# Attention and two feed-forward layers on one core: where the activation is made, and over how many units a weight's steps are spread

## The chip, the core and the metric

One core of a Trainium2 chip. It has five engines, each with an instruction queue of its own that is worked off in order: TensorE for matrix products (PE in the profile; PEld is its loading of weights), VectorE (DVE), ScalarE (ACT), GpSimd (POOL) and SyncE (SP, which here only issues transfers). Engines wait for one another by semaphores. TensorE writes to PSUM, in eight banks; all else lies in SBUF.

The metric is the device time of one execution in microseconds (us), lower being better. The kernel before was timed three times: 675.92, 677.68 and 681.2, median 677.68.

## The reference: what is computed

An attention of 2 batches, 12 heads, 448 tokens of 64, whose scores are mixed over the heads before the softmax and again after it, and then two feed-forward layers on the 896 tokens of 768:

```python
x = attn_out.transpose(0, 2, 1, 3).reshape(896, 768)
h = x @ w_in;  g = np.maximum(h, 0.0) + alpha * np.minimum(h, 0.0);  x = g @ w_out    # layer 1, d_ff 2048
h = x @ w_in2; g = np.maximum(0.01 * h, h);                          x = g @ w_out2   # layer 2
```

The weights arrive as float64, as two 32-bit words for each number, and are turned into float32 on the chip.

## The kernel before, in words

**Attention** takes the first 188 us of the profile. The order of its instructions on each engine is made by a planner (`Work`, with a table `STEPS` of costs and due times), which also places the first pieces of the feed-forward layers: the loading and splitting of the first weights and the first two output blocks of layer 1.

**Feed-forward** is worked in 80 units, written out in program order. A unit is one block of weights of 128 rows. Layer 1 has 16 up units (`u1_0` to `u1_15`, 768 columns, one block of 128 hidden features each, 36 matmuls of 448 tokens) and 24 down units (`d1_c_g`, 512 columns, 24 matmuls each; four of them make one output block `c` of 128 features); layer 2 has the same again. Each number is kept as a high part and a low part (`whi`, `wlo` for weights, `xhi`, `xlo` and `ghi`, `glo` for activations), and each product is made of three matmuls: `whi*xhi`, `whi*xlo`, `wlo*xhi`. In a group the first two kinds alternate (L449, L450), and the third kind follows (L452).

**The weights of a unit** need a load and seven steps, here called step 0 to step 6: the transfer `wraw` (L403, two buffers), step 0 on ScalarE (L418), steps 1 to 4 on VectorE (L420, L423, L425, L427), all in a working tile `wt` (two buffers), step 5 on ScalarE (L432), which makes `whi`, and step 6 on GpSimd (L435), which makes `wlo` (`whi` and `wlo` have two buffers). The same line serves up units (`wt_u`, 768 columns) and down units (`wt_d`, 512).

**The activation** of an up unit takes the sums `ps` (128x896, two banks of the four pairs of banks that take turns). In layer 1 VectorE makes `min(p,0)*alpha` into the tile `gt` (L606) and then adds `max(p,0)` (L608); in layer 2 ScalarE makes `0.01*p` (L610) and VectorE the maximum (L612). ScalarE then makes the high part `ghi` from `gt` (L614), GpSimd the low part `glo` (L615).

**The order around an up unit u**: VectorE gets the unit's own activation interleaved with steps 1 to 4 of unit u+2 (`prepare`), ScalarE its high part, step 0 of unit u+2 and step 5 of unit u+1, GpSimd step 6 of unit u+1 and `glo`, and SP the load of unit u+3. Steps 1 to 4 of unit u+2 and all that follows the matmuls of unit u stand in the same turn. In a down unit the group's matmuls stand ahead of the steps, and after each fourth one `to_y` (layer 1) or `to_out` (layer 2) takes the sums out.

Of the kernel before, what the change touches and what calls it, by code (L numbers as in the profile page):

```python
# [32 lines left out]
NCC, NFF = DM // 128, FF // 128  # L33
# [144 lines left out]
def tile_kernel(ctx: ExitStack, tc: tile.TileContext, qt, kt, vt, wmix, mmix,  # L178
# [3 lines left out]
    PE, DV, AC, PO, SP = nc.tensor, nc.vector, nc.scalar, nc.gpsimd, nc.sync  # L182
    PSUM = bass.MemoryType.PSUM

    const = ctx.enter_context(tc.tile_pool(name="const", bufs=1))
# [205 lines left out]
    raws, whl, wt = {}, {}, {}  # L391
# [5 lines left out]
    def load_w(e, u):  # L397
        if u >= len(units):
            return
        name, src = units[u]  # L400
        n = src.shape[-1]
        raw = pools["wp"].tile([128, 768, 2], I32, tag="wraw", name=f"wraw_{name}")
        e.dma_start(raw[:, :n], src.bitcast(I32).rearrange("p (n w) -> p n w", w=2))  # L403
        raws[u] = raw

    def split_w(e, u, i):

        if u >= len(units):
# [24 lines left out]
        if i == 6:  # L433
            hi, lo = whl[u]
            e.tensor_sub(lo[:, :n], t.bitcast(F32), hi[:, :n].bitcast(F32))  # L435

    SPLIT_ON = (AC, DV, DV, DV, DV, AC, PO)

    def three(p, whi, wlo, xhi, xlo, first, last):
        PE.matmul(p, whi, xhi, start=first, stop=False)  # L440
        PE.matmul(p, whi, xlo, start=False, stop=False)
        PE.matmul(p, wlo, xhi, start=False, stop=last)

    def group(p, whi, wlo, x, first, last):
# [38 lines left out]
    add(("load_mix",), 0, load_mix, wait=DMA)  # L483
    add(("clear",), 0, clear)
    add(("mixing",), 0, mixing, after=[("load_mix",)])

    for j, (b, t) in enumerate(tiles):
        start = first[j] - 20 if j else -40
        for c in range(NP2):
# [7 lines left out]
            p = "ps", "score", j, c  # L497
# [10 lines left out]
    for m, ks in enumerate(pairs):  # L508
        k0, k1 = ks[0], ks[-1]
        p, p2 = ("ps", "mix", m), ("ps", "post", m)  # L510
# [60 lines left out]
    def next_banks():  # L571
        n_bank[0] += 1
        return two_banks[in_turn[(n_bank[0] - 1) % NPS]]

    n_unit = [0]

    def prepare(i):

        u = n_unit[0]
        if i < 5:  # L580
            if u:
                split_w(SPLIT_ON[i], u + 2, i)
        elif u:
            if u > 1:
                split_w(SPLIT_ON[5], u + 1, 5)
                split_w(SPLIT_ON[6], u + 1, 6)
            load_w(SP, u + 3)

    def up(layer, x):
        g = []  # L590
        for f in range(NFF):
            whi, wlo = whl.pop(n_unit[0])
            ghi = gp.tile([128, B, S], F32R, tag=f"ghi{f}", name=f"ghi{layer}_{f}")
            glo = gp.tile([128, B, S], F32R, tag=f"glo{f}", name=f"glo{layer}_{f}")
            prepare(0)
            prepare(5)
            if layer == 1 and f in pu:
                p = pu[f]
            else:
                p = next_banks()  # L600
                for b in range(B):
                    group(p[:, b, :S], whi, wlo, list(zip(*x[b])), True, True)
            p = p[:, :, :S]
            t = gp.tile([128, B, S], F32, tag="gt", bufs=2, name=f"gt{layer}_{f}")
            if layer == 1:
                DV.tensor_scalar(t, p, 0.0, alpha_sb[:, f:f + 1], op0=ALU.min, op1=ALU.mult)  # L606
                prepare(1)
                DV.scalar_tensor_tensor(t, p, 0.0, t, op0=ALU.max, op1=ALU.add)  # L608
            else:
                AC.mul(t, p, 0.01)  # L610
                prepare(1)
                DV.tensor_max(t, p, t)  # L612
            prepare(2)
            AC.copy(ghi, t)  # L614
            PO.tensor_sub(glo, t, ghi.bitcast(F32))  # L615
            prepare(3)
            prepare(4)
            n_unit[0] += 1
            g.append((ghi, glo))
        return g  # L620

    def down(layer, g, done):
        for c in range(NCC):

            if layer == 2 and c == NCC - 1:
                p = [next_banks()[:, 0] for b in range(B)]
            else:
                both = next_banks()
                p = [both[:, b] for b in range(B)]
            for fg in range(4):  # L630
                whi, wlo = whl.pop(n_unit[0])
                prepare(5)
                for b in range(B):
                    group(p[b][:, :S], whi, wlo, [(hi[:, b], lo[:, b]) for hi, lo in g[4 * fg:4 * fg + 4]],
                          fg == 0, fg == 3)
                for part in range(5):
                    prepare(part)
                n_unit[0] += 1
            done(c, p)

    g = up(1, x)

    def to_y(c, p):
        for b in range(B):
            AC.copy(x[b][0][c], p[b][:, :S])
            DV.tensor_sub(x[b][1][c], p[b][:, :S], x[b][0][c].bitcast(F32))  # L646

    down(1, g, to_y)
    g = up(2, x)

    def to_out(c, p):
        o = gp.tile([128, B, S], F32, tag="gt", bufs=2, name=f"o_{c}")
        for b in range(B):
            AC.copy(o[:, b], p[b][:, :S])
            SP.dma_start(outT[128 * c:128 * c + 128, b * S:(b + 1) * S], o[:, b])
# [53 lines left out]
```

## Time and profile before

| | |
|---|---|
| median of three runs (lowest, highest) | 677.68 us (675.92, 681.2) |
| the profiled execution: its own time | 681.03 us |
| its span, first to last instruction | 679.0 us |
| PE busy | 644.0 us, 95% |
| DVE busy | 487.7 us, 72% |
| ACT busy | 273.8 us, 40% |
| POOL busy | 221.0 us, 33% |
| chain that ended last | PE 72%, DVE 19%, issue 4%, ACT 2% |
| TensorE's mean granted clock | 0.991 |

The profile is of one execution, by the chip's profiler. A busy share is an average over stages with different limits: the chain of waits, which is followed back from the last instruction, goes through PE nearly everywhere, but between 196 and 324 us, in the up units of layer 1, through DVE (the lines L606, L420, L425, L427). Matmuls overlap each other, so the start of one to the start of the next is what they cost, not the length of a row. In a row of the timeline the first number is the start in us from the span's start, the second the length; in brackets stands how long the engine had been idle before it and who ended that.

### The profile page before, as it was taken

To read this page: it belongs to the slowest core of one execution; us is meant where nothing else is said; L and a number is where in the kernel's file an instruction comes from. 1 tells how busy PE (TensorE), PEld (TensorE's weight loads), DVE (VectorE), ACT (ScalarE), POOL (GpSimd) and SP (SyncE) were. 2 spreads that over 40 slices of the span, in tenths; PEclk is the share of its full clock that TensorE was granted. 3 is DMA by queue.
4 is the path that set the end of the run, shared out by engine and by line. 5 is a ranking of instruction groups with operands and counts; after the bars stand their busy time and mean duration, and the time that the engine had idled before them with its cause. 6 is when DMAs were issued, how large, how long until landed. Compare 5 with 4: busy or idle time off the path is not lost.

```text
span 679.0 us, 14909 instructions
## 1 busy us (share of the span) xinstructions
PE 644.0 (95%) x6316; PEld 535.2 (79%) x6316; DVE 487.7 (72%) x589; ACT 273.8 (40%) x476; POOL 221.0 (33%) x174
## 2 busy tenths in 40 slices
PE   8879999999998888889899999999999999999997
PEld 3546656565797777778799999899899898999997
DVE  3758776788449999999666666667788776665651
ACT  4637656757323222222223232344454542323231
POOL 3101011102225444445323222245655553222221
PEclk9979999999999999999899999999999999999999
DMA  7668346333202222221333333422322323443430
GB/s 280 220 185 254 120 165 212 146 120 140 105 0 94 94 93 94 93 78 62 112 106 115 103 103 114 142 91 94 129 104 94 98 89 96 151 150 122 150 121 27
DMA packets 29189, 82.56 MB, mean 122 GB/s; under 512 B 2964, under 2 KB 15556, under 8 KB 29124
## 3 DMA queue, kind: packets, MB, share of 16 engines
q1 hardware_dynamic: 28692, 81.30, 36.1%
q8 instruction: 49, 0.80, 0.5%
q10 hardware_dynamic: 432, 0.33, 0.1%
q14 instruction: 16, 0.13, 0.1%
HBM read 59.51 MB, written 2.75 MB: 92 GB/s over the span
## 4 chain that ended last, share of the span: by engine, by line
PE 72%; DVE 19%; issue 4%; ACT 2%; DMA 1%; SPq 1%; POOL 1%; DVEq 0%; ACTq 0%; POOLq 0%
PE ps L449 17%; PE ps L452 17%; PE ps L450 16%; PE ps L335 6%; PE ps L370 6%; DVE wt_u L427 5%; PE ps L254 5%; PE ps L298 5%; DVE wt_u L420 4%; DVE gt L606 2%; DVE wt_u L425 2%; DVE wt_u L423 1%; DVE wt_d L427 1%; DMA k<-in_kt 1%; DVE stat L304 1%
## 5 line engine op out<-in xcount | busy, mean ns | idle before, releaser
L449 PE MATMUL ps<-xhi,whi_u 128*128 128x448 f32 x360 | 133.3, 370 | 13.8 <-ACT whi_u L432 13.8
L449 PE MATMUL ps<-ghi,whi_d 128*128 128x448 f32 x384 | 140.7, 366 | 3.8 <-ACT whi_d L432 3.8
L450 PE MATMUL ps<-glo,whi_d 128*128 128x448 f32 x384 | 140.3, 365 | 0.0
L450 PE MATMUL ps<-xlo,whi_u 128*128 128x448 f32 x360 | 131.1, 364 | 0.2 <-DVE xlo L646 0.2
L435 POOL TENSOR_TENSOR wlo_d<-wt_d,whi_d 128x512 fp32r<-128x512 f32 x48 | 62.1, 1293 | 156.3 <-ACT whi_d L432 116.6
L420 DVE TENSOR_SCALAR wt_d<-wt_d 128x512 f32<-128x512 f32 x48 | 52.2, 1087 | 61.1 <-ACT wt_d L418 61.1
L615 POOL TENSOR_TENSOR glo<-gt,ghi 128x896 fp32r<-128x896 f32 x32 | 74.8, 2339 | 61.5 <-ACT ghi L614 61.5
L452 PE MATMUL ps<-ghi,wlo_d 128*128 128x448 f32 x384 | 93.7, 366 | 0.0
L449 PEld LDWEIGHTS ps<-xhi,whi_u 128*128 128x128 f32 x360 | 67.5, 187 | 26.8 <-ACT whi_u L432 21.0
L435 POOL TENSOR_TENSOR wlo_u<-wt_u,whi_u 128x768 fp32r<-128x768 f32 x32 | 60.1, 1878 | 81.3 <-issue 50.7
L452 PE MATMUL ps<-xhi,wlo_u 128*128 128x448 f32 x360 | 82.6, 364 | 0.0
L449 PEld LDWEIGHTS ps<-ghi,whi_d 128*128 128x128 f32 x384 | 72.4, 189 | 10.7 <-ACT whi_d L432 4.9
L427 DVE SCALAR_TENSOR_TENSOR wt_u<-wraw_u,wt_u 128x768 int32<-128x768 int32 x32 | 77.7, 2429 | 1.0
L452 PEld LDWEIGHTS ps<-ghi,wlo_d 128*128 128x128 f32 x384 | 72.6, 189 | 5.9
L432 ACT CAST whi_d<-wt_d 128x512 fp32r<-128x512 f32 x48 | 29.8, 622 | 117.4 <-DVE wt_d L427 117.4
L450 PEld LDWEIGHTS ps<-glo,whi_d 128*128 128x128 f32 x384 | 72.4, 188 | 5.5
L335 PEld LDWEIGHTS ps<-wn,ex 60*64 60x64 f32 x2880 | 50.5, 136 | 28.3 <-issue 18.9
L450 PEld LDWEIGHTS ps<-xlo,whi_u 128*128 128x128 f32 x360 | 67.6, 188 | 5.5 <-DVE xlo L646 0.6
L452 PEld LDWEIGHTS ps<-xhi,wlo_u 128*128 128x128 f32 x360 | 67.5, 188 | 5.3
L321 POOL TENSOR_TENSOR wn<-wpost_sb,stat 128x120 f32<-128x120 f32 (+1 forms) x46 | 18.8, 411 | 147.2 <-DVE stat L316 95.9
L310 ACT ACTIVATE ex<-ps,stat 128x448 f32<-128x448 f32 x90 | 56.3, 636 | 14.7 <-DVE stat L304 14.4
L335 PE MATMUL ps<-wn,ex 60*64 60x60 f32 x2880 | 53.5, 221 | 8.9 <-issue 6.6
(53 smaller groups left out, 822.4 us busy)
## 6 DMA issues: line engine op xcount, KB each, us to landing
wraw_u<-in_win SPq DMA_DIRECT2D x32, 768.0 KB
wraw_d<-in_wout SPq DMA_DIRECT2D x48, 512.0 KB
kept<-stage SPq DMA_DIRECT2D x90, 210.0 KB
v<-in_vt SPq DMA_DIRECT2D x12, 256.0 KB
q<-in_qt SPq DMA_DIRECT2D x8, 360.0 KB
k<-in_kt SPq DMA_DIRECT2D x6, 448.0 KB
out_t<-o SPq DMA_DIRECT2D x12, 224.0 KB
mix<-in_wmix ACTq DMA_DIRECT2D x1, 156.0 KB
```

Of the source, the lines that this page charges most:

```text
L254: e.matmul(p[rows], qraw[j][mine, c, rows], kraw[b, c // KG][mine, c % KG], start=True, stop=True)
L298: e.matmul(p[HP * i:HP * i + HP, half], wpre_sb[mine], sraw[k][mine], start=True, stop=True)
L310: e.activation(ex[k], taken("mix", m)[:, i, :S], AF.Exp, bias=st[:, 0], scale=1.0, accum_out=st[:, 1])
L335: e.matmul(p[half][HP * beside:HP * beside + HP, c, :, b], a[mine, at:at + HP], w[mine, b], start=True, stop=True)
L370: e.matmul(p[64 * i:64 * i + 64], t[:, j, i], a[:, j, g, :n] if second else a2[:, j, :, g], start=j == 0, stop=j == NJ - 1)
L420: e.tensor_scalar_max(t.bitcast(F32), t.bitcast(F32), F64_FLOOR)
L427: e.scalar_tensor_tensor(t, least, 29, t, op0=ALU.logical_shift_right, op1=ALU.bitwise_or)
L435: e.tensor_sub(lo[:, :n], t.bitcast(F32), hi[:, :n].bitcast(F32))
L449: PE.matmul(p, whi[:, at[i]], xhi, start=first and i == 0, stop=False)
L450: PE.matmul(p, whi[:, at[i]], xlo, start=False, stop=False)
L452: PE.matmul(p, wlo[:, at[i]], xhi, start=False, stop=last and i == n - 1)
L615: PO.tensor_sub(glo, t, ghi.bitcast(F32))
```

## The change

The order of each turn is written anew, and some work moves between engines.

* The activation of unit u is done in the turn of unit u+1 (`pending` holds four functions for it: `negative`, `activate`, `high`, `low`).
* In layer 1 ScalarE makes the negative part in two instructions, `Relu(-p)` (L621) and a product with `less_alpha = -alpha` (L622); VectorE adds `max(p,0)` and writes the sum back into its PSUM banks (L628). In layer 2 ScalarE makes `0.01*p` as before (L624) and VectorE the maximum, back into the banks (L630). L606 is gone.
* `ghi` is made by ScalarE from the banks (L633). `glo` is made by VectorE from the banks (L636), no longer by GpSimd.
* The steps of a unit's weights are spread over three turns: in the turn of unit u VectorE does steps 1 to 4 of u+2, ScalarE step 5 of u+1 and step 0 of u+3, GpSimd step 6 of u+1, and SP issues the load of u+4. Steps 0 to 4 of unit 3 go to the planner.
* `to_y` and `to_out` run in the turn after their last group; `less_alpha` is made once, in `mixing`.

The order on TensorE stays as it was.

```diff
+    less_alpha = const.tile([128, NFF], F32, name="less_alpha")
...
     def mixing(e):
         DV.tensor_mul(mix, mix, same)
+        DV.tensor_scalar_mul(less_alpha, alpha_sb, -1.0)
...
-    for u in range(3):
-        for i in range(7):
-            later = 104 - u if u == 2 and i > 4 else 0
...
+    for u in range(4):
+        for i in range(7 if u < 3 else 5):
+            later = 103 if u == 3 else 104 - u if u == 2 and i > 4 else 0
+            free = [("split_w6", u - 2)] if u > 1 and i == 0 else [("up", 1, 0, NCC - 1)] if (u, i) == (2, 5) else []
...
+    def turn(fn, *args):
+        u = n_unit[0]
+        n_unit[0] += 1
+        steps = pending.pop(0) if pending else [lambda: None] * 4
+        steps[0]()
+        if u > 1:
+            split_w(AC, u + 1, 5)
+            split_w(PO, u + 1, 6)
+        fn(*whl.pop(u), *args)
+        if u > 1:
+            for i in range(1, 4):
+                split_w(DV, u + 2, i)
+        steps[1]()
+        steps[2]()
+        if u > 1:
+            split_w(DV, u + 2, 4)
+        steps[3]()
+        if u:
+            split_w(AC, u + 3, 0)
+        load_w(SP, u + 4)
...
-            if layer == 1:
-                DV.tensor_scalar(t, p, 0.0, alpha_sb[:, f:f + 1], op0=ALU.min, op1=ALU.mult)
-                prepare(1)
-                DV.scalar_tensor_tensor(t, p, 0.0, t, op0=ALU.max, op1=ALU.add)
-            else:
-                AC.mul(t, p, 0.01)
-                prepare(1)
-                DV.tensor_max(t, p, t)
-            prepare(2)
-            AC.copy(ghi, t)
-            PO.tensor_sub(glo, t, ghi.bitcast(F32))
...
+            def negative(p=p, t=t, f=f):
+                if layer == 1:
+                    AC.activation(t, p, AF.Relu, scale=-1.0)
+                    AC.mul(t, t, less_alpha[:, f:f + 1])
+                else:
+                    AC.mul(t, p, 0.01)
+
+            def activate(p=p, t=t):
+                if layer == 1:
+                    DV.scalar_tensor_tensor(p, p, 0.0, t, op0=ALU.max, op1=ALU.add)
+                else:
+                    DV.tensor_max(p, p, t)
+
+            def high(p=p, ghi=ghi):
+                AC.copy(ghi, p)
+
+            def low(p=p, ghi=ghi, glo=glo):
+                DV.tensor_sub(glo, p, ghi.bitcast(F32))
+
+            pending.append((negative, activate, high, low))
...
     def to_y(c, p):
-        for b in range(B):
-            AC.copy(x[b][0][c], p[b][:, :S])
-            DV.tensor_sub(x[b][1][c], p[b][:, :S], x[b][0][c].bitcast(F32))
+        def split():
+            for b in range(B):
+                AC.copy(x[b][0][c], p[b][:, :S])
+                DV.tensor_sub(x[b][1][c], p[b][:, :S], x[b][0][c].bitcast(F32))
+
+        return split, lambda: None, lambda: None, lambda: None
...
     down(2, g, to_out)
+    for steps in pending:
+        for step in steps:
+            step()
```

**On VectorE, in the turn of unit u1_4.** `wt_u_6` is the working tile of unit u1_6, `gt_4` the activation of unit u1_4, `gt_3` and `glo_3` those of unit u1_3; the last number of a name is that of its buffer. Before:

```order
L606 TENSOR_SCALAR gt_4_3157<-ps_63,alpha_sb 128x896
L420 TENSOR_SCALAR wt_u_6_3113<-wt_u_6_3113 128x768
L608 SCALAR_TENSOR_TENSOR gt_4_3157<-ps_63,gt_4_3157 128x896
L423 TENSOR_SCALAR wt_u_6_3113<-wt_u_6_3113 128x768
L425 SCALAR_TENSOR_TENSOR wt_u_6_3113<-wraw_u_6_3064,wt_u_6_3113 128x768
L427 SCALAR_TENSOR_TENSOR wt_u_6_3113<-wraw_u_6_3064,wt_u_6_3113 128x768
```

and now:

```order
L422 TENSOR_SCALAR wt_u_6_3111<-wt_u_6_3111 128x768
L425 TENSOR_SCALAR wt_u_6_3111<-wt_u_6_3111 128x768
L427 SCALAR_TENSOR_TENSOR wt_u_6_3111<-wraw_u_6_3057,wt_u_6_3111 128x768
L628 SCALAR_TENSOR_TENSOR ps_65<-ps_65,gt_3_3115 128x2x448
L429 SCALAR_TENSOR_TENSOR wt_u_6_3111<-wraw_u_6_3057,wt_u_6_3111 128x768
L636 TENSOR_TENSOR glo_3_3061<-ps_65,ghi_3_3060 128x896
```

Six instructions stand in a turn as before. The unit whose activation is made is one further back, L606 has gone, and `glo` has come.

**On ScalarE, at the same place.** Before, from the last instruction of the turn of u1_4 into that of u1_6:

```order
L614 CAST ghi_4_3111<-gt_4_3157 128x896
L418 ACTIVATE wt_u_7_3168<-wraw_u_7_3119 128x768
L432 CAST whi_u_6_3170<-wt_u_6_3113 128x768
L614 CAST ghi_5_3166<-gt_5_3212 128x896
L418 ACTIVATE wt_u_8_3223<-wraw_u_8_3174 128x768
```

and now:

```order
L621 ACTIVATE gt_3_3115<-ps_65 128x896
L622 ACTIVATE gt_3_3115<-gt_3_3115,less_alpha 128x896
L434 CAST whi_u_5_3120<-wt_u_5_3055 128x768
L633 CAST ghi_3_3060<-ps_65 128x896
L420 ACTIVATE wt_u_7_3167<-wraw_u_7_3113 128x768
```

This is the whole turn of u1_4. Step 5 of unit u1_5 now stands behind the negative part of unit u1_3, which waits for that unit's last matmul; the high part stands behind it.

**On VectorE, where attention ends.** `xlo` are the low parts of the attention's result, for which the first up units wait:

```order
L429 SCALAR_TENSOR_TENSOR wt_u_2_2737<-wraw_u_2_2711,wt_u_2_2737 128x768
L422 TENSOR_SCALAR wt_u_3_2865<-wt_u_3_2865 128x768
L425 TENSOR_SCALAR wt_u_3_2865<-wt_u_3_2865 128x768
L427 SCALAR_TENSOR_TENSOR wt_u_3_2865<-wraw_u_3_2824,wt_u_3_2865 128x768
L429 SCALAR_TENSOR_TENSOR wt_u_3_2865<-wraw_u_3_2824,wt_u_3_2865 128x768
L386 TENSOR_TENSOR xlo_75<-ps_64,xhi_73 128x2x200
```

The four steps of unit u1_3 now stand ahead of the last three blocks of `xlo`; before, they stood behind the activation of unit u1_0.

## Rows read from the trace of the kernel before

**Rows 1.** Busy time by stretch: stretch, its length, each engine's busy time, PEclk, DMA
```profile
324.90:329.40 4.50, 4.50 (x15) 4.04 (x16) 2.91 (x4) 1.37 (x3) 1.40 (x2) 0.62 0.39 117
329.40:438.00 108.60, 108.60 (x539) 100.70 (x538) 73.29 (x100) 31.88 (x55) 30.18 (x23) 1.00 0.38 119
675.50:679.00 3.50, 0.02 (x1) 0.00 (x0) 0.00 (x0) 0.53 (x1) 0.00 (x0) 0.78 0.18 66
```

**Rows 2.** Timeline of PE in the feed-forward layers: starts of matmul groups
```profile
198.29 0.36 PE L449 MATMUL ps<-xhi,whi_u 128*128 128x448 f32 x1
...
208.27 0.47 PE L449 MATMUL ps<-xhi,whi_u 128*128 128x448 f32 x1 [2.54 <-ACT whi_u L432]
...
310.07 0.47 PE L449 MATMUL ps<-xhi,whi_u 128*128 128x448 f32 x1 [1.02 <-ACT whi_u L432]
...
317.77 0.47 PE L449 MATMUL ps<-ghi,whi_d 128*128 128x448 f32 x1 [0.15 <-ACT whi_d L432]
...
324.89 0.47 PE L449 MATMUL ps<-ghi,whi_d 128*128 128x448 f32 x1 [2.00 <-ACT whi_d L432]
...
341.11 0.37 PE L449 MATMUL ps<-ghi,whi_d 128*128 128x448 f32 x1
...
343.54 0.37 PE L449 MATMUL ps<-ghi,whi_d 128*128 128x448 f32 x1
...
497.83 0.47 PE L449 MATMUL ps<-xhi,whi_u 128*128 128x448 f32 x1
...
512.64 0.47 PE L449 MATMUL ps<-xhi,whi_u 128*128 128x448 f32 x1
...
563.62 0.47 PE L449 MATMUL ps<-ghi,whi_d 128*128 128x448 f32 x1 [1.64 <-ACT whi_d L432]
```

**Rows 3.** Timeline of DVE in the turn of one up unit, layer 1
```profile
263.47 2.77 DVE L427 SCALAR_TENSOR_TENSOR wt_u<-wraw_u,wt_u 128x768 int32<-128x768 int32 x1
266.31 1.15 DVE L606 TENSOR_SCALAR gt<-ps,alpha_sb 128x896 f32<-128x896 f32 x1
267.38 2.18 DVE L420 TENSOR_SCALAR wt_u<-wt_u 128x768 f32<-128x768 f32 x1
269.47 1.08 DVE L608 SCALAR_TENSOR_TENSOR gt<-ps,gt 128x896 f32<-128x896 f32 x1
270.48 0.55 DVE L423 TENSOR_SCALAR wt_u<-wt_u 128x768 int32<-128x768 int32 x1
271.05 0.96 DVE L425 SCALAR_TENSOR_TENSOR wt_u<-wraw_u,wt_u 128x768 int32<-128x768 int32 x1
```

**Rows 4.** Timeline of POOL in the same turn
```profile
263.03 2.40 POOL L615 TENSOR_TENSOR glo<-gt,ghi 128x896 fp32r<-128x896 f32 x1 [2.47 <-ACT ghi L614]
267.30 1.84 POOL L435 TENSOR_TENSOR wlo_u<-wt_u,whi_u 128x768 fp32r<-128x768 f32 x1 [1.87 <-issue]
```

**Rows 5.** Timeline of DVE and of POOL in layer 2, an up unit
```profile
491.55 1.09 DVE L612 TENSOR_TENSOR gt<-ps,gt 128x896 f32<-128x896 f32 x1 [1.68 <-ACT gt L610]
...
490.39 1.85 POOL L435 TENSOR_TENSOR wlo_u<-wt_u,whi_u 128x768 fp32r<-128x768 f32 x1 [1.82 <-issue]
```

**Rows 6.** ACT by line, 445 to 555 us: busy us, mean ns | idle before
```profile
L610 ACT ACTIVATE gt<-ps 128x896 f32<-128x896 f32 x15 | 13.8, 919 | 6.5 <-PE ps L452 5.7
L418 ACT ACTIVATE wt_u<-wraw_u 128x768 f32<-128x768 f32 x13 | 11.8, 907 | 3.7 <-DMA wraw_u<-in_win 3.7
```

**Rows 7.** Timelines of DVE, SP's queue and ACT: a load and its step 0
```profile
165.62 0.95 DVE L427 SCALAR_TENSOR_TENSOR wt_u<-wraw_u,wt_u 128x768 int32<-128x768 int32 x1
...
166.67 10.80 SPq L403 DMA_DIRECT2D wraw_u<-in_win  x3
...
171.11 0.94 ACT L418 ACTIVATE wt_u<-wraw_u 128x768 f32<-128x768 f32 x1 [1.99 <-DMA wraw_u<-in_win]
```

**Rows 8.** Timeline of DVE where the feed-forward layers begin
```profile
183.65 0.79 DVE L384 TENSOR_TENSOR xlo<-ps,xhi 128x400 fp32r<-128x400 f32 x2 [6.58 <-ACT xhi L194]
...
196.13 1.15 DVE L606 TENSOR_SCALAR gt<-ps,alpha_sb 128x896 f32<-128x896 f32 x1 [6.02 <-PE ps L442]
```

**Rows 9.** DVE by line and form, 329.4 to 438 us, down units
```profile
L425 DVE SCALAR_TENSOR_TENSOR wt_d<-wraw_d,wt_d 128x512 int32<-128x512 int32 x21 | 14.5, 693 | 0.7
```

More of the change, by code (lines that the diff above doesn't have):

```diff
@@ L435, in split_w @@
             e.tensor_sub(lo[:, :n], t.bitcast(F32), hi[:, :n].bitcast(F32))
-    SPLIT_ON = (AC, DV, DV, DV, DV, AC, PO)
     def three(p, whi, wlo, xhi, xlo, first, last):
@@ L544, in tile_kernel @@
         add(("load_w", u), NB - 8 + u, load_w, wait=DMA, after=[("split_w4", u - 2) if u > 1 else ("weight_pools",)])
-    for u in range(3):
-        for i in range(7):
-            later = 104 - u if u == 2 and i > 4 else 0
-            free = [("split_w6", 0)] if (u, i) == (2, 0) else [("up", 1, 0, NCC - 1)] if (u, i) == (2, 5) else []
+    for u in range(4):
+        for i in range(7 if u < 3 else 5):
+            later = 103 if u == 3 else 104 - u if u == 2 and i > 4 else 0
+            free = [("split_w6", u - 2)] if u > 1 and i == 0 else [("up", 1, 0, NCC - 1)] if (u, i) == (2, 5) else []
             add((f"split_w{i}", u), NB - 5 + u + later, split_w, (u, i),
@@ L575, in tile_kernel, with up_group @@
     n_unit = [0]
-    def prepare(i):
+    pending = []
+    def turn(fn, *args):
         u = n_unit[0]
[L580 to L587, printed above, removed]
+        n_unit[0] += 1
[16 more added lines that the diff above has]
+        load_w(SP, u + 4)
+    def up_group(whi, wlo, p, x):
+        for b in range(B):
+            group(p[:, b, :S], whi, wlo, list(zip(*x[b])), True, True)
     def up(layer, x):
@@ L591, in up, with down_group @@
         for f in range(NFF):
-            whi, wlo = whl.pop(n_unit[0])
             ghi = gp.tile([128, B, S], F32R, tag=f"ghi{f}", name=f"ghi{layer}_{f}")
             glo = gp.tile([128, B, S], F32R, tag=f"glo{f}", name=f"glo{layer}_{f}")
-            prepare(0)
-            prepare(5)
             if layer == 1 and f in pu:
                 p = pu[f]
+                turn(lambda whi, wlo: None)
             else:
                 p = next_banks()
-                for b in range(B):
-                    group(p[:, b, :S], whi, wlo, list(zip(*x[b])), True, True)
+                turn(up_group, p, x)
             p = p[:, :, :S]
             t = gp.tile([128, B, S], F32, tag="gt", bufs=2, name=f"gt{layer}_{f}")
-            if layer == 1:
-                DV.tensor_scalar(t, p, 0.0, alpha_sb[:, f:f + 1], op0=ALU.min, op1=ALU.mult)
-                prepare(1)
-                DV.scalar_tensor_tensor(t, p, 0.0, t, op0=ALU.max, op1=ALU.add)
-            else:
-                AC.mul(t, p, 0.01)
-                prepare(1)
-                DV.tensor_max(t, p, t)
-            prepare(2)
-            AC.copy(ghi, t)
-            PO.tensor_sub(glo, t, ghi.bitcast(F32))
-            prepare(3)
-            prepare(4)
-            n_unit[0] += 1
+            def negative(p=p, t=t, f=f):
[14 more added lines that the diff above has]
+            pending.append((negative, activate, high, low))
             g.append((ghi, glo))
         return g
+    def down_group(whi, wlo, p, g, fg):
+        for b in range(B):
+            group(p[b][:, :S], whi, wlo, [(hi[:, b], lo[:, b]) for hi, lo in g[4 * fg:4 * fg + 4]], fg == 0, fg == 3)
     def down(layer, g, done):
@@ L630, in down @@
             for fg in range(4):
[L631 to L639, printed above, removed]
+                turn(down_group, p, g, fg)
+            pending.append(done(c, p))
     g = up(1, x)
     def to_y(c, p):
-        for b in range(B):
-            AC.copy(x[b][0][c], p[b][:, :S])
-            DV.tensor_sub(x[b][1][c], p[b][:, :S], x[b][0][c].bitcast(F32))
+        def split():
+            for b in range(B):
+                AC.copy(x[b][0][c], p[b][:, :S])
+                DV.tensor_sub(x[b][1][c], p[b][:, :S], x[b][0][c].bitcast(F32))
+        return split, lambda: None, lambda: None, lambda: None
     down(1, g, to_y)
@@ L651, in to_out, with leave @@
     def to_out(c, p):
[L652 to L655, printed above, removed]
+        def leave():
+            o = gp.tile([128, B, S], F32, tag="gt", bufs=2, name=f"o_{c}")
+            for b in range(B):
+                AC.copy(o[:, b], p[b][:, :S])
+                SP.dma_start(outT[128 * c:128 * c + 128, b * S:(b + 1) * S], o[:, b])
+        return leave, lambda: None, lambda: None, lambda: None
     down(2, g, to_out)
+    for steps in pending:
+        for step in steps:
+            step()
 def kernel(q, k, v, w_pre, w_post, moe_w_in, moe_w_out, moe_alpha, moe2_w_in, moe2_w_out):
```

## The prediction

> **What bounds the kernel now.** I read the chain of waits first: it goes through TensorE, except between 196 and 324 us, where it goes through VectorE. Then I measured what TensorE loses there and elsewhere.
>
> Its bare pace comes from a down stretch in which it was busy without a break [rows 1]: two half groups of 12 matmuls start 2.43 us apart [rows 2], so a matmul costs 0.2025 us, an up unit (36) 7.29 us and a down unit (24) 4.86 us. From the first matmul of unit u1_2 at 198.29 on [rows 2] there are 14x36 + 24x24 + 16x36 + 24x24 = 2232 matmuls, 452.0 us at that pace. They would end at 650.3 us; the last one ended at 675.5 [rows 1]. So 25.2 us are lost behind 198.29, and rows 2 show where:
> - u1_2 to the first down unit: 317.77 - 198.29 = 119.5 us for 504 matmuls, which need 102.1. Lost: 17.4. Each start waits for ScalarE's `whi`, 1.02 us by the row at 310.07, 2.54 at 208.27, besides a refill of the pipeline and the gap that is hidden in the length of the row before.
> - the first down unit: 324.89 - 317.77 = 7.1 instead of 4.86. Lost: 2.3.
> - 324.9 to 329.4: TensorE had stood for 2.0 us and its granted clock was 0.62 on average [rows 1], which mixes its levels of 2.4 and 1.2 GHz. Lost: 4.5 x 0.38 = 1.7.
> - layer 2's up units: two take 512.64 - 497.83 = 14.81 us, 7.405 each. Lost: 0.115 x 16 = 1.8.
> - into layer 2's down units, at 563.62: 1.64 and a refill. Lost: 1.7.
>
> That is 24.9; 0.3 is spread.
>
> Why `whi` is late: VectorE works without a pause in layer 1. One turn [rows 3] runs from 263.47 to about 272.0, 8.6 us, against TensorE's 7.29. Two of its six instructions are far too long. Step 4 (L427) takes 2.77 us, where the same instruction took 0.95 elsewhere [rows 7]; it began while GpSimd was in `glo` (263.03 to 265.43) and ended 0.8 us behind it [rows 4]. Step 1 (L420) takes 2.18, where its like, step 2, takes 0.55; it too ended 0.4 us behind GpSimd's step 6 [rows 3, 4]. So these two stand still while GpSimd works: 1.8 + 1.6 = 3.4 us of each turn. An instruction with one operand in PSUM does not: L612 ran for 1.09 us from 491.55, with GpSimd in step 6 until 492.24 [rows 5].
>
> **The change, part by part.** Take the turn of an up unit u, with T the moment when the matmuls of u-1 are done; TensorE begins u at about T.
>
> *ScalarE, layer 1.* The negative part reads PSUM like L610, 0.92 us [rows 6]. The product with `less_alpha` is 896 long, where L418 takes 0.907 for 768 [rows 6]: at most 1.06, I take 1.0. So `gt` is ready at T+1.9. Step 5 follows, at most 0.9: `whi` of u+1 at T+2.8. TensorE wants it at T+7.29: 4.5 us to spare, where it was late before. GpSimd's step 6, 1.84 [rows 4], is done at T+4.65; it is wanted 12 matmuls into u+1, at T+9.7.
>
> *VectorE.* L606 (1.15 [rows 3]) goes. `activate` is L608 with its output in PSUM, and no row has VectorE writing there. Bounds: 1.08 as L608, and 2.77, the longest row of any such instruction [rows 3]; I take 1.08, since inputs, length and operation are the same. It ends at T+3.0. Step 4 then meets GpSimd until T+4.65 and ends at T+5.6. `high` on ScalarE ends at T+3.95. `low` is like L612, 1.09 [rows 5], bounded above by the same 2.77: T+6.7. ScalarE's step 0 of u+3 waits for step 6 of u+1 (the working tile) and ends at T+5.6, so steps 1 to 3 of u+3 (0.55 + 0.55 + 0.96 [rows 3]) run at once, to T+8.75. The next `activate` cannot start before T+7.29+1.9 = T+9.2. So VectorE's turn is 8.75 - 1.9 = 6.85 us, 0.44 below TensorE's 7.29: TensorE sets the pace, and the 17.4 go. Of GpSimd's two holds one is left, 1.65 us long.
>
> *Layer 2.* Without the product everything is 1.0 earlier against T and the turn the same 6.85: the 1.8 go. VectorE gets `low` besides, 1.09 in each of 16 turns; the hold by `glo`, 1.8, pays for it.
>
> *Into the down units.* Step 5 no longer follows step 4 in one turn, so the 2.3 and the 1.7 go; with the stop goes the slow clock behind it, 1.7.
>
> *Down units.* Steps 3 and 4 take 0.69 [rows 9], steps 1 and 2 at most 0.55: 2.5 us in 4.86. In the turn behind a finished block ScalarE copies twice and VectorE subtracts in between, ahead of step 5: below 0.92 + 1.09 + 0.92, with step 5 T+3.8 at the latest, wanted at T+4.86. Hidden; if it were late by all of it, under 3 us, 5 times a layer.
>
> *Start.* Steps 1 to 4 of u1_3 (3.0 us) move into VectorE's pause of 6.6 us before 183.65 [rows 8]; a load takes 4.4 us (166.67 to 171.1 [rows 7]), so they may be late by some tenths, and then push `xlo`. From 196.1 [rows 8] ScalarE does step 5 of u1_2, both negative parts, a `high` and a step 0 in turn with one `activate`: about 0.8 + 1.9 + 1.1 + 1.0 + 0.9 + 1.9 + 0.9 = 8.5, so `whi` of u1_3 comes at 204.6, wanted at 198.29 + 7.29 = 205.6. Bounds: 0 and 3.0; I take 0.5. `less_alpha`, 16 numbers wide, and the moved output transfers cost nothing I can find; VectorE and the queue wait there anyway.
>
> *The sum.* 25.2 back, less 0.5 for the start and 0.5 for refills at the seams: 24.2. The profiled execution took 681.03 us, 3.35 above the median of 677.68. Against the median: 677.68 - 24.2 = **653.5 us**.
>
> **Two rules of the skill.** The Trainium skill (VectorE: DVE Perf Modes, section Rules for kernel authors) speaks against the change: with many operations on a matmul's output one should copy it from PSUM to SBUF first. By the rows PSUM costs nothing extra: 1.09 us for 896 is 1.22 ns an element [rows 5], 0.96 for 768 in SBUF 1.25 [rows 3]. By the rule alone the sum would lean towards rival A. The other one, the Trainium skill (SBUF — State Buffer, section Who interferes with whom), says that a VectorE instruction with at most one SBUF input and outside the two-port modes does not contend with GpSimd; by it rival A falls away. Rows 5 agree, for an output in SBUF.
>
> **The rivals.**
>
> *A. GpSimd holds the new instructions too.* For it: no row has a PSUM output, and VectorE is near its limit. Then `activate` starts at T+4.65, when step 6 is done, and ends at T+5.75, step 4 at 6.7, `low` at 7.8, steps 1 to 3 at 9.85: a turn of 7.95, 0.66 over TensorE's, in 30 units 19.8 us: 673 us. Against it: L612 [rows 5]. Smaller surcharges give times between; from 0.44 us a turn it decides.
>
> *B. The loads come late, and the kernel gets slower.* The load of u+4 is issued when step 4 of u+2 frees its buffer, and in two turns it must land and pass steps 0 to 4. In a down unit that is the landing L + 0.7 + 2.5 + 0.1 for issue, in 2 x 4.86 = 9.72: it decides from L = 6.4 us. At L = 8 each of 48 units loses 0.8 us: 38, or 691 us. For it: in layer 2 step 0 already waits for a load now and then [rows 6]. Against it: a load of an up unit, half as large again, takes 4.4 [rows 7].
>
> *C. The seams keep their stops.* The first units and the passages into down units wait as now in part: 4 to 8 of the 25 us stay, 657 to 661.
>
> **How the numbers follow.** My forecast has 0.78 (651 to 657; the runs shown differ by 0.8%), C 0.08, A 0.10, B 0.04. About 1% is what a measurement of this kernel can tell, 6.8 us: faster is below 670.9. All of the forecast and of C and half of A lie there: 0.91; the rest of A 0.05 within 1%; slower 0.04, B. The range 649.5 to 663 takes in the forecast, C and the cheaper part of A.
>
> **What would show it.** Right: up units of layer 1 start 7.3 us apart; TensorE's idle time before L449 is close to nothing; step 1 at 0.55 us in layer 1, and in an up unit only step 4 is longer than 1.1; `activate` and `low` about 1.1; no stretch of clock below 1.0 near the first down units. Wrong: `activate` or `low` at 1.7 or more (A), step 0 waiting for loads by microseconds in the down units (B), idle marks on PE at the seams (C).

## The result, and the profile after

| | before | changed | ratio, 95% interval |
|---|---|---|---|
| first timing | 678.71 us | 662.47 us (658.44 to 666.63) | 0.975 (0.970 to 0.980) |
| second timing | 680.75 us | 656.56 us (653.87 to 662.22) | 0.966 (0.962 to 0.970) |
| third timing | 678.96 us | 654.78 us (652.44 to 662.5) | 0.962 (0.959 to 0.966) |

The kernel is faster, by 16 to 24 us. The forecast was 653.5, with 649.5 to 663.0 as the range. The first timing has a fourth run of the kernel before (679.74), hence 678.71 and not 677.68. The second and third timing are of the same changed kernel; how far their difference from the first can be explained is told below. Ratios leave out executions more than 1.5% above the fastest of their timing (two of four of order_alone, whose other two took 655.51 and 660.49 us, and one of six of the third timing, of late_alpha, of glo_back and of early_q11), while medians and ranges count them.

The profiled execution took 658.44 us, 22.6 less than the one before. The page's chain of waits now reads:

```profile
PE 92%; DVE 3%; DMA 2%; issue 1%; ACT 1%; POOL 1%; SPq 0%; POOLq 0%; DVEq 0%; ACTq 0%
```

It was 72% PE and 19% DVE. The timeline of TensorE, at the places of [rows 2] (units u1_2, u1_3 and u1_7, the first two half groups of the down units, the second layer, its down units, the end):

```profile
200.43 0.37 PE L449 MATMUL ps<-xhi,whi_u 128*128 128x448 f32 x1
...
207.73 0.36 PE L449 MATMUL ps<-xhi,whi_u 128*128 128x448 f32 x1
...
236.91 0.37 PE L449 MATMUL ps<-xhi,whi_u 128*128 128x448 f32 x1
...
302.58 0.36 PE L449 MATMUL ps<-ghi,whi_d 128*128 128x448 f32 x1
...
305.01 0.36 PE L449 MATMUL ps<-ghi,whi_d 128*128 128x448 f32 x1
...
419.31 0.37 PE L449 MATMUL ps<-xhi,whi_u 128*128 128x448 f32 x1
...
536.18 0.36 PE L449 MATMUL ps<-ghi,whi_d 128*128 128x448 f32 x1
...
652.11 0.98 PE L452 MATMUL ps<-ghi,wlo_d 128*128 128x448 f32 x4
```

No row carries a bracket any more: from 200.43 on TensorE waits for nothing. An up unit takes 207.73 - 200.43 = 7.30 us, a half group of a down unit 2.43. From 200.43 to the end (652.11 + 4 x 0.2025 = 652.92) are 452.5 us, against 452.0 at the bare pace and 477.1 before. I call these 452.5 us **the stretch**; it is the sharpest measure here. A second profile of the changed kernel has 452.5 again, while whole times scatter by more than 10; a third has 457.0, with TensorE at a slower pace through all of layer 2 (after_third, below). The clock no longer falls into the first down units, where [rows 1] had 0.62 (in each row the bounds and the length, then the busy time of TensorE, of its loading of weights, of VectorE, ScalarE and GpSimd, the granted clock, and DMA):

```profile
302.58:307.08 4.50, 4.50 (x24) 4.18 (x23) 2.28 (x2) 3.61 (x5) 1.29 (x1) 1.00 0.06 25
307.08:419.00 111.92, 111.92 (x554) 103.87 (x553) 81.95 (x104) 34.29 (x56) 35.93 (x23) 1.00 0.36 116
```

One turn of VectorE in layer 1, in place of [rows 3]:

```profile
239.14 1.10 DVE L628 SCALAR_TENSOR_TENSOR ps<-ps,gt 128x896 f32<-128x896 f32 x1 [0.74 <-ACT gt L622]
240.15 2.47 DVE L429 SCALAR_TENSOR_TENSOR wt_u<-wraw_u,wt_u 128x768 int32<-128x768 int32 x1
242.54 1.08 DVE L636 TENSOR_TENSOR glo<-ps,ghi 128x896 fp32r<-128x896 f32 x1
243.54 0.54 DVE L422 TENSOR_SCALAR wt_u<-wt_u 128x768 f32<-128x768 f32 x1
244.12 0.56 DVE L425 TENSOR_SCALAR wt_u<-wt_u 128x768 int32<-128x768 int32 x1
244.72 0.96 DVE L427 SCALAR_TENSOR_TENSOR wt_u<-wraw_u,wt_u 128x768 int32<-128x768 int32 x1
246.45 1.10 DVE L628 SCALAR_TENSOR_TENSOR ps<-ps,gt 128x896 f32<-128x896 f32 x1 [0.77 <-ACT gt L622]
```

and GpSimd's and ScalarE's part of it:

```profile
239.96 1.84 POOL L437 TENSOR_TENSOR wlo_u<-wt_u,whi_u 128x768 fp32r<-128x768 f32 x1 [5.44 <-ACT whi_u L434]
```

```profile
237.11 0.92 ACT L621 ACTIVATE gt<-ps 128x896 f32<-128x896 f32 x1 [1.64 <-PE ps L452]
238.06 1.05 ACT L622 ACTIVATE gt<-gt,less_alpha 128x896 f32<-128x896 f32 x1
239.01 0.82 ACT L434 CAST whi_u<-wt_u 128x768 fp32r<-128x768 f32 x1
```

The turn lasts 246.45 - 239.14 = 7.31 us, TensorE's own; 0.77 of it VectorE waits. Only step 4 (L429) is still long: it ends at 242.6, 0.8 behind GpSimd's step 6. `whi` of the next unit is ready at 239.8, and its unit began at 236.91 + 7.29 = 244.2.

### The profile page after: what moved, and what is told of

It reads as the page before. It is cut to its first block, busy times and chain, and to the rows that moved or that the text cites. A ratio compares the mean times of both kernels' runs of the same rounds, so it can differ in the third digit from the quotient of the medians.

```text
span 656.6 us, 14914 instructions
## 1 busy us (share of the span) xinstructions
PE 637.9 (97%) x6316; PEld 534.8 (81%) x6316; DVE 464.9 (71%) x606; ACT 305.6 (47%) x508; POOL 152.8 (23%) x142
## 4 chain that ended last, share of the span: by engine, by line
PE 92%; DVE 3%; DMA 2%; issue 1%; ACT 1%; POOL 1%; SPq 0%; POOLq 0%; DVEq 0%; ACTq 0%
PE ps L450 23%; PE ps L452 23%; PE ps L449 23%; PE ps L337 6%; PE ps L372 6%; PE ps L255 5%; PE ps L300 4%; DMA q<-in_qt 1%; DVE stat L306 1%; DMA k<-in_kt 1%; PE ps L442 1%; PE ps L440 1%; DVE a L194 1%; PE ps L441 1%; ACT ex L312 0%
## 5 line engine op out<-in xcount | busy, mean ns | idle before, releaser
L449 PE MATMUL ps<-xhi,whi_u 128*128 128x448 f32 x360 | 131.6, 365 | 0.0
L437 POOL TENSOR_TENSOR wlo_d<-wt_d,whi_d 128x512 fp32r<-128x512 f32 x48 | 68.3, 1424 | 171.3 <-ACT whi_d L434 73.7
L420 ACT ACTIVATE wt_d<-wraw_d 128x512 f32<-128x512 f32 x48 | 32.2, 671 | 82.8 <-DMA wraw_d<-in_wout 40.9
L429 DVE SCALAR_TENSOR_TENSOR wt_u<-wraw_u,wt_u 128x768 int32<-128x768 int32 x32 | 66.2, 2067 | 0.2
L422 DVE TENSOR_SCALAR wt_d<-wt_d 128x512 f32<-128x512 f32 x48 | 21.4, 445 | 51.0 <-ACT wt_d L420 50.9
L429 DVE SCALAR_TENSOR_TENSOR wt_d<-wraw_d,wt_d 128x512 int32<-128x512 int32 x48 | 55.0, 1145 | 1.4
L306 DVE TENSOR_REDUCE stat<-ps 128x2 f32<-128x896 f32 (+1 forms) x46 | 48.6, 1066 | 9.2 <-PE ps L300 7.6
```

The lines of the kernel that those rows point to most:

```text
L306: e.reduce_max(stat[m][:, 0, :n], taken("mix", m)[:, :n, :S], axis=AX, negate=True)
```

## The experiments

Each kernel was timed beside the kernel before on the same chip. First a table by the parts of the change, then each kernel:

| kernel | order of the steps | negative part | `glo` | activation in | stretch, us |
|---|---|---|---|---|---|
| before (two profiles) | old | VectorE | GpSimd | SBUF | 477.1, 476.5 |
| glo_alone | old | VectorE | VectorE | SBUF | 470.7 |
| order_alone | new | VectorE | GpSimd | SBUF | 459.1 |
| glo_back | new | ScalarE | GpSimd | SBUF | 452.4 |
| neg_vector | new | VectorE | VectorE | PSUM | 452.6 |
| in_sbuf | new | ScalarE | VectorE | SBUF | 452.7 |
| changed (three profiles) | new | ScalarE | VectorE | PSUM | 452.5, 452.5, 457.0 |
| order_back | step 5 behind step 4 | ScalarE | VectorE | PSUM | 457.6 |

**glo_alone**

```diff
-            PO.tensor_sub(glo, t, ghi.bitcast(F32))
+            DV.tensor_sub(glo, t, ghi.bitcast(F32))
```

> The kernel before with one edit: the low part glo is made by VectorE instead of GpSimd. Theory that it takes both, the move of glo and the weights' steps a turn further ahead: step 4 is back at about 1 us, but step 5 of a unit still follows its step 4 at once and step 6 then meets step 1 of the next turn; an up unit of layer 1 takes about 8.1 us instead of 8.57, the whole 670 to 674. Rival 1, glo on GpSimd is all of it: up units at 7.3 us, 657 to 662. Rival 2, VectorE is simply full (one instruction of 1.1 us more in a turn of 8.6): slower than before, 680 to 693.

Measured: 673.62 us, ratio 0.989 (0.986 to 0.992); up units 8.28 us apart. The numbers of the first theory hold, those of the rivals don't; that it takes both edits falls below, where glo_back does without the move of `glo`. VectorE's turn:

```profile
240.99 1.15 DVE L606 TENSOR_SCALAR gt<-ps,alpha_sb 128x896 f32<-128x896 f32 x1 [0.29 <-PE ps L452]
242.06 1.96 DVE L420 TENSOR_SCALAR wt_u<-wt_u 128x768 f32<-128x768 f32 x1
243.94 1.08 DVE L608 SCALAR_TENSOR_TENSOR gt<-ps,gt 128x896 f32<-128x896 f32 x1
244.94 0.54 DVE L423 TENSOR_SCALAR wt_u<-wt_u 128x768 int32<-128x768 int32 x1
246.03 1.09 DVE L615 TENSOR_TENSOR glo<-gt,ghi 128x896 fp32r<-128x896 f32 x1 [0.55 <-ACT ghi L614]
247.04 0.95 DVE L425 SCALAR_TENSOR_TENSOR wt_u<-wraw_u,wt_u 128x768 int32<-128x768 int32 x1
248.03 0.96 DVE L427 SCALAR_TENSOR_TENSOR wt_u<-wraw_u,wt_u 128x768 int32<-128x768 int32 x1
249.25 1.15 DVE L606 TENSOR_SCALAR gt<-ps,alpha_sb 128x896 f32<-128x896 f32 x1 [0.27 <-PE ps L452]
```

and ScalarE's step 5 with the start of TensorE's unit behind it:

```profile
249.07 0.83 ACT L432 CAST whi_u<-wt_u 128x768 fp32r<-128x768 f32 x1 [2.27 <-DVE wt_u L427]
```

```profile
249.96 0.47 PE L449 MATMUL ps<-xhi,whi_u 128*128 128x448 f32 x1 [0.74 <-ACT whi_u L432]
```

VectorE now has 0.8 us to spare in each turn, and TensorE still waits 0.74 for `whi`. So it is not VectorE's sum that binds, but a loop: a unit's last matmul releases L606; steps 1 to 4 stand behind it, step 5 behind step 4, and TensorE's next unit behind step 5. The loop takes 8.28 us, 1.4 of them a hold of step 1 (1.96 instead of 0.55) by GpSimd's step 6 (241.75 to 243.60), which starts as step 5 ends (241.62).

**glo_back** (the changed kernel, with)

```diff
-                    DV.scalar_tensor_tensor(p, p, 0.0, t, op0=ALU.max, op1=ALU.add)
+                    DV.scalar_tensor_tensor(t, p, 0.0, t, op0=ALU.max, op1=ALU.add)
...
-                DV.tensor_sub(glo, p, ghi.bitcast(F32))
+                PO.tensor_sub(glo, t, ghi.bitcast(F32))
```

and `ghi` and layer 2's maximum likewise with `t`.

> The changed kernel with the activation in the SBUF tile gt and glo on GpSimd again; the order of the weights' steps and the negative part on ScalarE stay as changed. Theory that the distance of step 4 from step 5 is what counts: step 4 stands still until GpSimd is done with step 6 and glo (about 4.3 us from its start instead of 2.4), VectorE's turn becomes 7.3 us, just TensorE's, and whi is made a turn later: 0 to 4 us slower than the changed kernel. Rival, the standing still decides by itself: a turn of 8.0 us, 0.7 x 30 = 20 us slower, about 683.

Measured: 657.96 us, 0.969 (0.964 to 0.973), against 656.56 of the changed kernel beside it; stretch 452.4. The theory holds in its result; where VectorE stands still it had wrong: not step 4 for 4.3 us (its mean is 1.28), but steps 1 and 3 (means of 1.97 and 1.87 us). VectorE by line, 204 to 298 us (busy us, mean ns, idle before):

```profile
L422 DVE TENSOR_SCALAR wt_u<-wt_u 128x768 f32<-128x768 f32 x11 | 21.7, 1969 | 6.5 <-ACT wt_u L420 6.5
L427 DVE SCALAR_TENSOR_TENSOR wt_u<-wraw_u,wt_u 128x768 int32<-128x768 int32 x11 | 20.6, 1869 | 0.4
```

With the new order, standing still behind GpSimd costs nothing here, where VectorE still gets through a turn in TensorE's 7.3 us.

**neg_vector** (the changed kernel, with)

```diff
-                    AC.activation(t, p, AF.Relu, scale=-1.0)
-                    AC.mul(t, t, less_alpha[:, f:f + 1])
+                    DV.tensor_scalar(t, p, 0.0, alpha_sb[:, f:f + 1], op0=ALU.min, op1=ALU.mult)
```

> The changed kernel with layer 1's negative part on VectorE again, min(p,0)*alpha in one instruction as before the change. Theory: VectorE has 0.74 us to spare in a turn, and its activation no longer waits 1.9 us for ScalarE, so that step 6 lies under instructions that read PSUM and holds step 4 less; turn 6.8 us, below 7.29: the feed-forward stretch (first matmul of u1_2 to the end) stays at 452.4 us. Rival: the 1.07 us come on top of 6.57 + 0.74, turn 7.64 to 7.9 in 14 units, 457 to 461.

Measured: 657.85 us, 0.967 (0.963 to 0.971); stretch 452.6, as the theory had it, though the turn was 7.5 us, not 6.8: GpSimd's step 6 now falls on step 1 (1.82 us). VectorE falls 0.2 us behind in each turn, 3 us in 14, and the turn by which its steps are ahead takes that up.

**in_sbuf** is glo_back with `glo` on VectorE.

> The changed kernel with the activation written into the SBUF tile gt instead of its PSUM bank; ghi and glo are made from there, glo on VectorE. Theory: where the result lies costs and gives nothing; the activation 1.08, glo 1.1, stretch 452.4 us. Rival: glo now has both operands in SBUF and stands still under step 6 like step 4; in the worst case VectorE's turn is 1.8 longer, 8.4 us, and the stretch 475 us or more.

Measured: 657.54 us, 0.965 (0.960 to 0.970); stretch 452.7. VectorE by line, 204 to 302 us:

```profile
L636 DVE TENSOR_TENSOR glo<-gt,ghi 128x896 fp32r<-128x896 f32 x15 | 16.2, 1079 | 1.0 <-ACT ghi L633 1.0
L628 DVE SCALAR_TENSOR_TENSOR gt<-ps,gt 128x896 f32<-128x896 f32 x14 | 15.3, 1090 | 9.6 <-ACT gt L622 9.6
```

1.08 and 1.09 us, as with PSUM (1.08 and 1.10). Keeping the activation in its bank brings no time. `glo` with both operands in SBUF isn't held here, since GpSimd is done before it starts; whether it would be, this kernel doesn't show.

**order_alone** has neg_vector's edit on top of glo_back: only the order is new.

> The new order of the weights' steps and nothing else: negative part on VectorE and glo on GpSimd as before the change, activation in gt. Theory that the order is what counts, since step 5 stands a turn behind step 4 and VectorE's own sum is then the only limit: its six instructions take 6.2, and two stretches of GpSimd hold them 1 to 2 us; turn 7.3 to 7.9 in layer 1, 7.3 in layer 2; stretch 453 to 462 us. Rival, it takes glo off GpSimd as well: a turn of 8.4 as before the change, stretch 470 us or more.

Measured: 664.81 us, 0.966 (0.960 to 0.972); stretch 459.1: the order alone brings 18.0 of the 24.6 us. VectorE, one turn and the next:

```profile
243.01 1.15 DVE L621 TENSOR_SCALAR gt<-ps,alpha_sb 128x896 f32<-128x896 f32 x1
244.07 1.76 DVE L422 TENSOR_SCALAR wt_u<-wt_u 128x768 f32<-128x768 f32 x1
245.87 2.08 DVE L425 TENSOR_SCALAR wt_u<-wt_u 128x768 int32<-128x768 int32 x1
247.99 0.96 DVE L427 SCALAR_TENSOR_TENSOR wt_u<-wraw_u,wt_u 128x768 int32<-128x768 int32 x1
248.86 1.08 DVE L627 SCALAR_TENSOR_TENSOR gt<-ps,gt 128x896 f32<-128x896 f32 x1
249.86 0.95 DVE L429 SCALAR_TENSOR_TENSOR wt_u<-wraw_u,wt_u 128x768 int32<-128x768 int32 x1
250.73 1.15 DVE L621 TENSOR_SCALAR gt<-ps,alpha_sb 128x896 f32<-128x896 f32 x1
```

and TensorE where the up units end:

```profile
304.49 0.48 PE L449 MATMUL ps<-ghi,whi_d 128*128 128x448 f32 x1 [0.56 <-ACT whi_d L434]
307.02 1.08 PE L452 MATMUL ps<-ghi,wlo_d 128*128 128x448 f32 x4 [0.63 <-POOL wlo_d L437]
311.08 0.47 PE L449 MATMUL ps<-ghi,whi_d 128*128 128x448 f32 x1 [0.55 <-ACT whi_d L434]
313.61 1.09 PE L452 MATMUL ps<-ghi,wlo_d 128*128 128x448 f32 x4 [0.64 <-POOL wlo_d L437]
```

VectorE is the slower one, 7.72 us a turn without a pause, and yet TensorE loses nearly nothing (0.9 us) in the 14 up units: VectorE's lag of 0.43 x 14 = 6 us eats its lead and comes due in the first three down units, with 3.6 us. Another 2.0 us of this stretch are a pace of 2.48 instead of 2.43 us a half group in the rest of layer 1's down units. No row shows its cause, and the changed kernel has the same pace in one of its profiles (after_third), so it is not shown to come from this order; without it the order alone would bring some 20 us, by estimate (18.0 + 2.0).

**order_back** (the changed kernel, with)

```diff
         if u > 1:
-            split_w(DV, u + 2, 4)
+            split_w(DV, u + 1, 4)
+            split_w(AC, u + 1, 5)
+            split_w(PO, u + 1, 6)
```

with steps 1 to 3 of u+1, step 0 of u+2 and the load of u+3 in the turn of u.

> The changed kernel with step 5 and step 6 of a unit right behind its step 4 in the same turn, one unit less ahead; activation in PSUM, glo on VectorE and negative part on ScalarE stay as changed. Theory of the loop: what counts is the time from a unit's last matmul to whi of the unit after the next, and here only negative, activation, step 4 and step 5 stand in it, 4.9 us of 7.29: stretch 452.4 to 455 us. Rival, step 5 must be a turn behind step 4: up units at 7.6 us or more and stops at the first down units, stretch 460 us or more.

Measured: 659.93 us, 0.970 (0.964 to 0.976); stretch 457.6. Between the two: up units run at 7.29, so a step 5 right behind step 4 does no harm there, as the theory of the loop has it. But the first unit takes 8.34 us instead of 7.30, and in the turn behind each of the five output blocks (x) 0.7 us are lost. TensorE, the first two of five, 20.26 us apart, a block's length:

```profile
323.93 0.47 PE L449 MATMUL ps<-ghi,whi_d 128*128 128x448 f32 x1 [0.53 <-ACT whi_d L434]
...
344.19 0.47 PE L449 MATMUL ps<-ghi,whi_d 128*128 128x448 f32 x1 [0.54 <-ACT whi_d L434]
```

VectorE and ScalarE ahead of the first:

```profile
320.36 0.62 DVE L663 TENSOR_TENSOR xlo<-ps,xhi 128x448 fp32r<-128x448 f32 x1 [0.60 <-ACT xhi L662]
...
322.54 0.69 DVE L429 SCALAR_TENSOR_TENSOR wt_d<-wraw_d,wt_d 128x512 int32<-128x512 int32 x1
```

```profile
323.26 0.62 ACT L434 CAST whi_d<-wt_d 128x512 fp32r<-128x512 f32 x1 [2.94 <-DVE wt_d L429]
```

Taking out the block stands in the same queue ahead of steps 1 to 5. That the steps are a turn further ahead is what pays in the down units: 4.1 us. This edit moves all seven steps and the load; what the place of step 5 alone is worth there it doesn't show.

**after_again, before_again**: the two kernels once more.

> The changed kernel once more, for a second profile. Theory: from the first matmul of u1_2 to the end of the last one TensorE again needs 452 to 454 us (2232 x 0.2025), and what differs between executions (658.4 to 666.6 so far) lies ahead of it, in attention; ratio to before 0.965 to 0.980. Rival: the feed-forward stretch itself differs between executions (a late load, a stretch at a lower granted clock); then a profile that is slower than 660 shows more than 455 us there.

> The kernel before once more, for a second profile. Theory: its feed-forward stretch is 476 to 478 us as in the first profile, the first matmul of u1_2 lies between 195.5 and 201 us. Rival, attention is faster there than in the changed kernel: below 195.5.

Measured: changed 656.56 us, stretch 452.5 from 198.84; before 675.21 in one run, stretch 476.5 from 192.89. Both stretches repeat. In the second profile of the kernel before the granted clock stays at 1.00 behind the stop at the first down units, and layer 1's down units take 118.9 us instead of 120.4. Its clock is at 0.50 elsewhere, from 203.0 to 206.4, behind a stop of 2.54 us at 202.87, and its first three up units take 27.1 us instead of 26.1. Each of the three profiles with the old order has one such stretch behind one of its stops (glo_alone from 209.1 to 212.5), and none of the eleven with the new order has one in its stretch. So the place of the 1.7 us of [rows 1] belongs to that execution; a low clock behind a stop, for 1.0 us here and 1.6 there, both profiles of the kernel before have. Attention's end, at 192.9 to 204.9 in 14 profiles, is what scatters; the rival of before_again, attention being faster before the change, has one profile for it (192.89) and two against it (198.29, and 198.67 in glo_alone), while the new order has 195.54 too (order_back).

**late_alpha, early_q5, early_q11**: two edits at attention, the second on top of the first, with -5 or -11.

```diff
     def mixing(e):
-        DV.tensor_scalar_mul(less_alpha, alpha_sb, -1.0)
...
         fn(engines.get(e), *args)
+    DV.tensor_scalar_mul(less_alpha, alpha_sb, -1.0)
```

```diff
-    "load_q": (-2, dict(S=1.0)),
+    "load_q": (-5, dict(S=1.0)),
```

> less_alpha is made behind attention instead of between the first two VectorE instructions. Theory: at the start VectorE waited 1.34 us for the alpha transfer and the first softmax came 1.8 us later (18.69 instead of 16.89); with the move it is back at about 16.9, and the time is 0.8 to 1.8 us less than that of the changed kernel. Rival: the wait for the q load at 43.6 us (4.68 us) takes the lead away again: within 0.5 us of the changed kernel.

> The changed kernel with less_alpha behind attention and the due time of the q loads 3 units earlier (-5 instead of -2): the load for which TensorE waited 4.68 us at 43.6 is issued 3 transfers earlier. Theory that the differing times hang on that wait: about 3 x 0.85 us earlier at the queue, the wait falls below 2 us, the median is 1 to 3 us below the changed kernel's beside it, and the times lie closer together than its 12.8 us. Rival: another transfer takes its place (the kept blocks behind it come later), the median within 1 us or higher.

> The same with the due time 9 units earlier (-11): the load is issued 9 transfers earlier, some 7 us. Theory: no wait for q at 40 us any more, median 2 to 4 us below the changed kernel's. Rival: the transfers compete in the first 40 us, in which the DMA engines are busy for 0.70 to 0.76 of the time, so the softmax blocks come later by the load's length: within 1 us or up to 3 us higher.

Measured: 659.43, 658.37 and 657.09 us, against 656.56 (late_alpha) and 654.78 of the changed kernel beside them. None is faster; all three theories fall. The rivals of the two with the q load moved hold (3.6 and 2.3 us above the changed kernel), but with times that scatter by 9 to 13 us these differences are not clear of noise. Without `less_alpha` in the way the first softmax still comes at 18.47 us (18.69 with it, VectorE waiting 1.34 us for alpha): TensorE's scores were late themselves, below. With the q load earlier TensorE no longer waits for it, and yet the times go from 653.5 to 662.9 and from 652.2 to 662.3.

**after_third** served as the measure of these two.

> The changed kernel a third time, as the measure for the other kernels timed beside it. Theory that its spread comes from attention's first 50 us: stretch from the first matmul of u1_2 again 452.4 us, that matmul between 195.5 and 201 us, ratio to before 0.962 to 0.976.

The ratio is 0.962 (0.959 to 0.966). The profiled execution, 662.5 us, has a stretch of 457.0 us: layer 2 runs at 2.48 us a half group from its first unit to its end, at a granted clock of 1.00 and without a wait. TensorE at the start of the stretch, of layer 2, of its down units, and at the end:

```profile
200.01 0.37 PE L449 MATMUL ps<-xhi,whi_u 128*128 128x448 f32 x1
...
418.89 0.37 PE L449 MATMUL ps<-xhi,whi_u 128*128 128x448 f32 x1
...
537.95 0.37 PE L449 MATMUL ps<-ghi,whi_d 128*128 128x448 f32 x1
...
656.16 0.99 PE L452 MATMUL ps<-ghi,wlo_d 128*128 128x448 f32 x4
```

So the theory on the stretch falls in this execution, and the rival of after_again, that the stretch itself differs between executions, holds in one profile of three. What slows TensorE there is open.

No kernel tried beats the changed one: 0.5 us is left between its stretch and the bare pace.

## Why the prediction was right, and where it was not

**The loss of TensorE** was placed and sized right. 25.2 us were counted (25.1 if the end is taken from the last row's start, as in the other profiles), 24.6 came back (477.07 - 452.49), 24.2 were forecast. The 0.5 for refills and the 0.5 for the start were not needed: `whi` of u1_3 came 1.5 us before its unit.

**The turn of VectorE** came out as worked out: `activate` 1.10 and `low` 1.08 (1.08 and 1.09 taken), step 4 done 5.7 us behind T (242.6 - 236.9; 5.6 forecast), 6.54 us of work (6.85). In down units steps 3 and 4 take 0.88 and 1.22 instead of 0.69, as GpSimd's step 6 now overlaps them; they had 4.86 - 2.5 to spare.

**Rival A** falls: with GpSimd's step 6 at work from 211.88 to 213.77, `activate` at 211.99 took 1.09 us with its output in PSUM. Here the Trainium skill (SBUF — State Buffer, section Who interferes with whom) and the trace agree; what comes nearest to its other rule, copying to SBUF first (VectorE: DVE Perf Modes, section Rules for kernel authors), is in_sbuf, and it makes no difference here: 452.7 against 452.5. **Rival B**: ScalarE's step 0 does wait for loads in down units, 36.3 us in all before 21 of them, so the sign named for it is there; but it hides, and the stretch shows none of it. **Rival C**: no seam stops.

**What was right for a reason too narrow.** I gave the 17.4 us of layer 1 to instructions that stand still, 3.4 us of each turn, and the cure to VectorE's shorter sum. Standing still was the smaller part of it. With the same two GpSimd stretches and a VectorE turn of 7.7 us the order alone brings 18.0; with one of the two holds gone (`glo`'s, on step 4) and the old order it is 6.4. The new order, which I priced for the seams alone ("Step 5 no longer follows step 4 in one turn"), though the T+2.8 of `whi` rests on it, is the main part: it takes steps 1 to 5 out of the loop through `whi`. order_back leaves steps 4 and 5 in it, the loop is short enough for up units, and only the first unit and the turns behind finished blocks lose. On top of the order either relief does, ScalarE's negative part (452.4) or VectorE's `glo` (452.6); both together are not needed, and the PSUM bank isn't either.

**The time.** In the profiled pair: 24.6 back, 2.1 lost by attention ending at 200.43 instead of 198.29 (1.8 of it there already at the first softmax, 18.69 against 16.89), 0.15 back in what lies around: 22.6. The first timing's median is 9.0 us above the forecast and near the edge of its range. The second and third gained 24.2 each, the forecast's size. The profiles show two things that differ between executions and that the sum took as fixed: attention's end (198.84 to 200.43 in the changed kernel's three, 192.9 to 204.9 in all) and, in one of the three, TensorE's pace in layer 2 (4.5 us). Of the first timing's slower three executions there is no profile, so which of the two made them slower stays open. The term that was drawn too narrow is "the start": its 0.5 us with bounds 0 and 3.0 covered the first up units, where nothing was lost, and left out that attention's end moves by several us from one execution to the next. That the first timing still fell into the range owes something to the room kept for rivals C and A, which did not come true.

## What to carry to other kernels

An engine without a pause in the chain of waits need not be the bound by its sum: follow what its queue waits for and what waits for it, and if that closes a loop through the engine that should never stop, take one step out of the loop by working a unit further ahead. A lead of one unit also lets an engine run a few per cent too slow for as long as the lead lasts, and the bill comes at the next stage. Of a change in four parts, try them apart: here the order carried three quarters, either of two other parts gave the rest, and the place of the result gave nothing.

## What the runs showed that was not expected

TensorE's first scores. In the three profiles with the old order, the first 96 matmuls on k and q (from 6.1 us) took 9.24 us; in the eleven of the changed kernel and its variants 10.6 to 12.2. One us of it, before and late_alpha (columns as above):

```profile
8.00:9.00 1.00, 1.00 (x16) 0.53 (x12) 0.33 (x1) 0.88 (x2) 0.00 (x0) 1.00 1.03 401
```

```profile
8.00:9.00 1.00, 1.00 (x12) 0.50 (x8) 0.00 (x0) 0.59 (x1) 0.00 (x0) 0.50 1.03 398
```

The granted clock is 0.50 there (7.0 to 10.4 us), that is 1.2 instead of 2.4 GHz, although late_alpha gives every engine the same instructions up to there. It had risen to 1.00 at 3.6 us, during TensorE's first eight matmuls, and fell after TensorE had stood for 1.98 us; in the profile before it reads 1.00 from 5.1 us on, and the 1.78 us for which TensorE stood brought no fall. In other profiles the half pace comes earlier (glo_back: 8 matmuls from 8.00 to 9.00), and the trace has a record of the clock only from where it ends (8.9 us); the 1.00 of such a row says nothing. The 96 matmuls take 1.3 to 3 us longer by it. How much of that reaches the end of attention no run shows, and why it comes with the new programs stayed open.

GpSimd is held as well. Where VectorE's steps 1 and 2 overlap it, GpSimd's step 6 takes 2.16 us instead of 1.84 (order_alone, at 245.38), and in the down units of the changed kernel 1.54 instead of 1.29:

```profile
L437 POOL TENSOR_TENSOR wlo_d<-wt_d,whi_d 128x512 fp32r<-128x512 f32 x23 | 35.4, 1538 | 78.3 <-ACT whi_d L434 32.1 <-DVE xlo L664 28.6 <-PE ps L452 17.7
```
